# Sixteen engines for w_down's 32 single rows, and a narrow strip of the first values in seven small loads

## The chip, the cores and the metric

The kernel runs on one core of a Trainium2 chip. A core has TensorE (PE in the profile; its weight loads PEld), VectorE (DVE), ScalarE (ACT), GpSimd (POOL) and SyncE (SP), which here only issues transfers, and sixteen DMA engines that carry them out. The metric is the time of one execution on the device in microseconds, the median of several runs.

## The reference

One token of 512 numbers is normalised and goes through two branches in parallel, whose outputs are added to it. All inputs are float32.

```python
xn = layernorm(x)                                   # (1, 1, 512)
# A: attention on a cache, 32 heads of 128, 4096 positions
q = (xn @ wq).reshape(1, 1, 32, 128).transpose(0, 2, 1, 3)
p = softmax(einsum("bhqd,bhkd->bhqk", q, k_cache) * 128 ** -0.5)
a = einsum("bhqk,bhkd->bhqd", p, v_cache) ... .reshape(1, 1, 4096) @ wo
# B: one routed token (the sequence has one), feed-forward width 1376
r = xn @ w_r
y = (silu(xn @ w_gate) * (xn @ w_up)) @ w_down
b = xn + y * sigmoid(r)
return x + a + b
```

The two caches hold 67 MB each; with the weights, 159.5 MB are read once.

## The kernel before

The 32 heads are worked off in eight groups of four. A group's keys (K) and values (V) are 8.39 MB each, 16384 numbers or 64 KB on each of 128 partitions: a partition holds 128 positions of one head. `load_group` (lines 99 to 104) issues such a load as one transfer. Its source is taken apart as `b g p h (c d)`: 32 shares of positions (p) of four heads (h), so that the outermost size of a transfer is 32 and partition 4p + h gets share p of head h.

VectorE and GpSimd multiply keys by the query in place (lines 253, 269) and sum them (264, 271); the softmax's maximum goes over TensorE (324); TensorE multiplies the probabilities by the values, 64 instructions per group (348). There are two places for keys and values in the SBUF: `ring`, with three slots of half a group, for keys of groups 1 to 7 and the last values, and `vals`, with one group, for the keys of group 0 and then for the values of groups 0 to 6. So values g can be loaded once values g-1 are used up, and keys g once VectorE has summed the first half of keys g-1.

All large loads are issued by SyncE in the order in which the program is written: w_q, 32 rows of w_down, keys 0, w_gate and w_up in halves, keys 1, then values g-1 behind keys g, and at the end values 7, the rest of w_down, and w_o in six pieces. A load that is issued waits on each of the sixteen engines behind what was issued earlier.

The framework gives each load one of eight semaphores in turn, DMAHW0 to DMAHW7 (the two tiny loads of x and w_r on ScalarE's queue take part). A load that gets a semaphore again waits on SyncE until the load that had it before has landed; where this is long past, the wait doesn't show in the order of instructions or costs nothing. Waits are also added where a load overwrites something (on the load that wrote it, and on the engines that read it: PE, DVE).

w_down has 1376 rows. The last 1344 are loaded in one piece at the end (`load_down`, line 123). The first T = 32 are loaded at line 133 as single rows into the tile `wf`, one row of 2 KB on each of 32 partitions. `FEW` = 4 sets the outermost size of that transfer's source, `(b a) n -> a b n` with a = 4, and with it which row lies on which partition; lines 296 to 299 put the 32 hidden values that go with them in the same order. TensorE uses both at line 405, near the end.

The main loop (lines 432 to 475) issues keys g and values g-1 ahead of the work on them:

```python
    for g in range(NG + 1):
        if 0 < g < NG:
            K[g] = load_keys(g)
            V[g - 1] = load_group(v_cache, g - 1, vals)
        elif g:
            V[g - 1] = load_group(v_cache, g - 1, ring[:, SLOT:SLOTS * SLOT])
```

Of the kernel before, what the change touches and what calls it, by code (L numbers as in the profile page):

```python
# [14 lines left out]
HP = 4  # L15
# [3 lines left out]
NP = 24  # L19
G = 4  # L20
NCOL = 4
PARTS = (16,), (8, 4, 2.5, 1, 0.5)
T = 32
FEW = 4


@with_exitstack
def kernel(
# [13 lines left out]
    nc = tc.nc  # L42
    _, H, Sk, Dh = k_cache.shape
# [3 lines left out]
    PP = P // HP  # L47
# [5 lines left out]
    RB = BH * Dh // P  # L53
    TH = BH // NCOL
    DC = D // NCOL
    FT = (F - T) // NCOL
    FP = (F - T) * D // P
    QR = NCOL * (F - T) // P
    NS = -(-QR // NCOL)
    OFF = [QR * a // NCOL for a in range(HP)]  # L60
    QC = QB * Dh
# [19 lines left out]
    vals = const.tile([P, 2 * SLOT], F32, name="vals")  # L81
# [14 lines left out]
        halves(t, w.rearrange("(p j) f -> p (j f)", p=P))  # L96
        return [t[:, j * F:(j + 1) * F] for j in range(NK)]

    def load_group(cache, g, t, c0=0):

        n = t.shape[1]
        src = cache[0].rearrange("(b h g) (p c) d -> b g p h (c d)", b=NB, g=GB, p=PP)[g // GB, g % GB]
        nc.sync.dma_start(t, src[:, :, c0 * Dh:c0 * Dh + n])
        return t.rearrange("p (c d) -> p c d", d=Dh)

    def load_keys(g):

        i = (1 - g % 2) * SLOT
        t = load_group(k_cache, g, ring[:, i:i + 2 * SLOT] if g else vals)
        t = [t[:, :HC], t[:, HC:]]  # L110
        return [(h, t[h]) for h in ((1, 0) if g % 2 else (0, 1))]

    def load_wo(t, b, parts):
        src = wo[b * BH * Dh:(b + 1) * BH * Dh, :].rearrange("(p r) n -> p (r n)", p=P)
        x = 0
        for n in parts:
            y = x + int(n * D)
            nc.sync.dma_start(t[:, x:y], src[:, x:y])  # L118
            x = y
        return t.rearrange("p (r n) -> p r n", n=D)  # L120

    def load_down(t):
        nc.sync.dma_start(t, w_down[T:].rearrange("f n -> (f n)").rearrange("(p x) -> p x", p=P))
        return t
# [7 lines left out]
    WF = const.tile([T, D], F32, name="wf")  # L132
    nc.sync.dma_start(WF, w_down[:T].rearrange("(b a) n -> a b n", a=FEW))  # L133
    K, V = {0: load_keys(0)}, {}
# [89 lines left out]
    for j in range(NK):  # L224
        for i in range(NQ * HP):
            t, k = i % NCOL, i // HP
# [12 lines left out]
    def q_part(k):  # L239

        ps = ps_q.tile([P, QB, Dh], F32, name="q")
        nc.tensor.matmul(ps.rearrange("p g d -> p (g d)"), pick.rearrange("p i h -> p (i h)"), q_sb[:, k, :],
                         start=True, stop=True)

        nc.scalar.activation(q_sb[:, k, :], ps.rearrange("p g d -> p (g d)"), AF.Copy)
        return ps
# [4 lines left out]
    def multiply(g, i, c0, c1):  # L251
        q, k = Q[g // QB][:, g % QB, :], K[g][i][1]
        nc.vector.tensor_tensor(  # L253
            k[:, c0:c1, :], k[:, c0:c1, :],
            q[:, None, :].to_broadcast([P, c1 - c0, Dh]), op=ALU.mult
        )

    def sums(g, i):
        if i == 0:
            S[g] = small.tile([P, C], F32, name="s")  # L260
        h, k = K[g][i]
        s = S[g][:, h * HC:(h + 1) * HC]
        for c, n in ((slice(0, HC - NP), Dh), (slice(HC - NP, HC), Dh // 2)):
            nc.vector.tensor_reduce(s[:, c], k[:, c, :n], axis=AX.X, op=ALU.add)  # L264

    def rest(g, i):

        k, q = K[g][i][1][:, HC - NP:], q_sb[:, g // QB, :].rearrange("p (g d) -> p g d", d=Dh)[:, g % QB, :]
        nc.gpsimd.tensor_tensor(k, k, q[:, None, :].to_broadcast([P, NP, Dh]), op=ALU.mult)  # L269
        a, b = k[:, :, :Dh // 2], k[:, :, Dh // 2:]  # L270
        nc.gpsimd.tensor_tensor(a, a, b, op=ALU.add)  # L271
# [18 lines left out]
    def ffn_hidden():  # L290
# [5 lines left out]
        nc.vector.scalar_tensor_tensor(  # L296
            hr[:, NS + 1].rearrange("p (a b) -> p a b", a=FEW), hid[:, :T].rearrange("p (b a) -> p a b", a=FEW), sr,
            up[:, :T].rearrange("p (b a) -> p a b", a=FEW), op0=ALU.mult, op1=ALU.mult,
        )
# [18 lines left out]
    def own_max(g):  # L318
        m = small.tile([P, 1], F32, name="m")
        nc.vector.reduce_max(m, S[g], axis=AX.X)  # L320
        dg = small.tile([P, PP], F32, name="dg")
        nc.vector.tensor_scalar(dg, fold, m, SCALE, op0=ALU.mult, op1=ALU.mult)  # L322
        ps = ps_s.tile([P, 512], F32, name="ps_small")
        nc.tensor.matmul(ps[:, :PP], same.rearrange("p i h -> p (i h)"), dg, start=True, stop=True)  # L324
        MX[g] = ps[:, :PP]

    def head_max(g):
        nm = small.tile([P, 1], F32, name="nm")
        nc.vector.tensor_reduce(nm, MX.pop(g), axis=AX.X, op=ALU.max, negate=True)  # L329
        MX[g] = nm  # L330

    def expo(g):
        nm, s = MX.pop(g), S.pop(g)
        if g % GB == 0:
            RS[g // GB] = small.tile([P, GB], F32, name="rs")
        e = small.tile([P, C], F32, name="e")
        nc.scalar.activation(e, s, AF.Exp, bias=nm, scale=SCALE, accum_out=RS[g // GB][:, g % GB:g % GB + 1])  # L337

        nc.gpsimd.tensor_tensor(PT[g % 2], e[:, :, None].to_broadcast([P, C, HP]),  # L339
                                mine[:, None, :].to_broadcast([P, C, HP]), op=ALU.mult)  # L340

    def values(g):

        v, p, ps = V.pop(g), PT[g % 2], ps_pv[g % 2]
        ng = C // G
        for i in range(ng):
            r = 32 * (i % NCOL)
            nc.tensor.matmul(  # L348
                ps[r:r + M, :], p[:, G * i:G * (i + 1), :].rearrange("p c h -> p (c h)"),
                v[:, G * i:G * (i + 1), :].rearrange("p c d -> p (c d)"),  # L350
                start=(i < NCOL), stop=(i >= ng - NCOL),
            )
# [17 lines left out]
    def turn(b, den):  # L370

        rinv = small.tile([P, TH], F32, name="rinv")
        nc.vector.reciprocal(rinv, den[:, :TH])  # L373
        o = late[2].rearrange("p (r i) -> p r i", r=RB)
        nc.vector.tensor_tensor(
            o.rearrange("p r (k i) -> p k i r", k=TH),
            ps_o.rearrange("p (k i r) -> p k i r", k=TH, r=RB),
            rinv[:, :, None, None].to_broadcast([P, TH, Dh // RB, RB]), op=ALU.mult,
        )
        ot = late[b].rearrange("p (r i) -> p r i", r=RB)  # L380
        nc.vector.transpose(ot.rearrange("p r i -> p (r i)"), o.rearrange("p r i -> p (r i)"))
        OT[b] = ot
# [49 lines left out]
    for g in range(NG + 1):  # L432
        if 0 < g < NG:
            K[g] = load_keys(g)
            V[g - 1] = load_group(v_cache, g - 1, vals)
        elif g:

            V[g - 1] = load_group(v_cache, g - 1, ring[:, SLOT:SLOTS * SLOT])

            WD = load_down(vals[:, :FP])  # L440
            WO = [load_wo(vals[:, SLOT:], 0, PARTS[0]), load_wo(ring[:, :SLOT], 1, PARTS[1])]
            acc = ps_q.tile([P, QB, Dh], F32, name="q").rearrange("p g d -> p (g d)")
            down = ps_q.tile([P, QB, Dh], F32, name="q").rearrange("p g d -> p (g d)")
            for t in (acc, down):
                nc.vector.memset(t, 0.0)
            nc.vector.tensor_copy(acc[0:1, :], base)
        if g:
            own_max(g - 1)
        n = (HC - NP) // 2
        if 0 < g < NG:  # L450
            rest(g, 0)
            multiply(g, 0, 0, n)
        if g:
            head_max(g - 1)
            expo(g - 1)
        if (g + 1) % QB == 0 and (g + 1) // QB < NQ:
            Q[(g + 1) // QB] = q_part((g + 1) // QB)
        if g < NG:
            rest(g, 1)
            if g:  # L460
                multiply(g, 0, n, HC - NP)
                sums(g, 0)
            multiply(g, 1, 0, HC - NP)
            sums(g, 1)
            if DEN:
                turn(*DEN.popitem())
        if g:
            values(g - 1)
            keep(g - 1)
            if g == 1:  # L470
                HL, HF = ffn_hidden()
            if g == NG:
                sb = rows_down()
            if g % GB == 0:
                DEN[g // GB - 1] = collect(g // GB - 1)
# [3 lines left out]
    rows = [(OT[b][:, r, 0:1], WO[b][:, r, :]) for b in range(NB) for r in range(RB)]  # L479
    n = len(rows) - RB + PARTS[1][0]  # L480
    for j, (lhsT, rhs) in enumerate(rows[:n]):
# [6 lines left out]
    for j, (lhsT, rhs) in enumerate(rows[n:-2]):  # L488
        if j == PARTS[1][1]:
            gather(sb, first[:, 0, 0, 0:1])  # L490
# [40 lines left out]
```

## Time and profile before

| | us |
|---|---|
| median of three runs (376.7 to 376.88) | 376.82 |
| the profiled execution | 377.09 |
| its span, first to last instruction | 375.3 |

| engine | busy us | share of the span |
|---|---|---|
| TensorE | 118.3 | 32% |
| VectorE | 228.3 | 61% |
| GpSimd | 172.2 | 46% |
| ScalarE | 16.1 | 4% |

159.45 MB were read, 425 GB/s over the span; the 3814 packets of SyncE's loads took 98.4% of the time of sixteen engines.

In the profile's lists a row gives the line of the kernel, the engine and the operation, then the tile written and those read. In a timeline row the first number is the start, the second the length, both in us from the span's start; "SPq" is SyncE issuing a transfer, and the bracket says how long the engine stood idle before and what ended that. A window row gives the window, its length, each engine's busy time (and instructions), the granted clock of TensorE, and last the share of the sixteen DMA engines' time taken by the packets that begin in the window, and their bytes in GB/s. Since a packet counts where it begins, a share can be above 1.

### The profile page before, as it was taken

What the parts mean: (1) busy time and instruction counts of PE and PEld (TensorE: products, weight loads), DVE (VectorE), ACT (ScalarE), POOL (GpSimd) and SP (SyncE); (2) the same over time, 40 slices, a digit from 0 to 9 for tenths busy, and PEclk for the clock granted to TensorE, in tenths of its full rate; (3) what the DMA queues carried; (4) which work ended last, traced back from release to release, by engine and by line L of the source; (5) the groups of instructions that cost most, each with busy time, mean ns of one, the idle gap of its engine ahead of it and who ended that gap; (6) DMA issues with size and microseconds to landing.
All of it is one profiled execution on the core that took longest, in us unless ns stands there. A gap on an engine that the chain in (4) does not pass through costs nothing.

```text
span 375.3 us, 2071 instructions
## 1 busy us (share of the span) xinstructions
PE 118.3 (32%) x850; PEld 34.9 (9%) x850; DVE 228.3 (61%) x132; ACT 16.1 (4%) x37; POOL 172.2 (46%) x56
## 2 busy tenths in 40 slices
PE   1156045000810063005300490036002700190995
PEld 1101011000200011001000130001000100020222
DVE  6300499389867990699159924995299419970020
ACT  3001000000010000100000000000000000000001
POOL 2000497089407950696059703980299019911000
PEclk9999565555675568556855597559555955575899
DMA  8999899999998999999999999999999999998995
GB/s 336 447 454 447 370 449 447 447 447 440 426 440 385 440 442 433 447 447 447 426 419 405 440 442 433 447 447 435 433 419 420 440 433 433 440 442 387 437 419 219
DMA packets 3826, 159.57 MB, mean 425 GB/s; under 512 B 455, under 2 KB 583, under 8 KB 874
## 3 DMA queue, kind: packets, MB, share of 16 engines
q1 hardware_dynamic: 3814, 159.45, 98.4%
q8 instruction: 6, 0.10, 0.1%
q14 instruction: 2, 0.02, 0.0%
q10 hardware_dynamic: 4, 0.00, 0.0%
HBM read 159.45 MB, written 0.00 MB: 425 GB/s over the span
## 4 chain that ended last, share of the span: by engine, by line
DMA 74%; PE 17%; DVE 7%; SPq 1%; issue 0%; ACT 0%; DVEq 0%
DMA vals<-in_A_v_cache_dram 55%; PE ps_pv L348 17%; DMA vals<-in_A_k_cache_dram 11%; DMA ring<-in_A_wo_dram 9%; DVE s L264 4%; DVE vals L253 3%; SPq L118 0%; PE ps_acc L428 0%; SPq L133 0%; PE ps_small L324 0%; SPq L84 0%; PE ps_o L428 0%; ACT res L499 0%; DVE nm L329 0%; PE ps_pv L428 0%
## 5 line engine op out<-in xcount | busy, mean ns | idle before, releaser
L269 POOL TENSOR_TENSOR ring<-ring,q_sb 128x3072 f32<-128x3072 f32 x14 | 93.6, 6685 | 116.8 <-DMA ring<-in_A_k_cache_dram 116.8
L348 PE MATMUL ps_pv<-vals,pt 128*16 128x512 f32 x448 | 63.0, 726 | 189.4 <-DMA vals<-in_A_v_cache_dram 189.4
L253 DVE TENSOR_TENSOR ring<-ring,q 128x2560 f32<-128x2560 f32 (+1 forms) x21 | 77.8, 3702 | 71.0 <-DMA ring<-in_A_k_cache_dram 71.0
L264 DVE TENSOR_REDUCE s<-ring 128x40 f32<-128x5120 f32 (+1 forms) x28 | 100.0, 3614 | 0.8
L271 POOL TENSOR_TENSOR ring<-ring 128x1536 f32<-128x1536 f32 x14 | 48.1, 3436 | 1.1
L348 PEld LDWEIGHTS ps_pv<-vals,pt 128*16 128x16 f32 x448 | 15.0, 112 | 232.5 <-issue 232.5
L269 POOL TENSOR_TENSOR vals<-vals,q_sb 128x3072 f32<-128x3072 f32 x2 | 13.4, 6689 | 37.6 <-DMA vals<-in_A_k_cache_dram 37.6
L253 DVE TENSOR_TENSOR vals<-vals,q 128x5120 f32<-128x5120 f32 x2 | 11.0, 5483 | 28.3 <-DMA vals<-in_A_k_cache_dram 28.3
L264 DVE TENSOR_REDUCE s<-vals 128x40 f32<-128x5120 f32 (+1 forms) x4 | 14.3, 3614 | 0.1
L373 DVE RECIPROCAL rinv<-ps_small 128x4 f32<-128x4 f32 x2 | 0.4, 178 | 21.5 <-PE ps_small L364 21.5
L227 PE MATMUL ps_pv<-ring,xnT 128*1 128x512 f32 x64 | 9.9, 783 | 10.5 <-DMA ring<-in_A_wq_dram 10.5
L357 ACT ACTIVATE pv<-ps_pv 128x512 f32<-128x512 f32 x8 | 4.8, 597 | 191.5 <-PE ps_pv L348 191.5
L339 POOL TENSOR_TENSOR pt<-e,mine 128x512 f32<-128x512 f32 x8 | 8.3, 1040 | 8.7 <-ACT e L337 8.7
L348 PE MATMUL ps_pv<-ring,pt 128*16 128x512 f32 x64 | 8.4, 687 | 9.4 <-DMA ring<-in_A_v_cache_dram 9.4
L279 PE MATMUL ps_acc<-ring,xnT 128*1 128x336 f32 (+1 forms) x32 | 4.2, 678 | 15.4 <-DMA ring<-in_B_w_gate_dram 15.4
L337 ACT ACTIVATE e<-s,nm 128x128 f32<-128x128 f32 x8 | 3.2, 402 | 120.2 <-DVE nm L329 120.2
L324 PE MATMUL ps_small<-dg,same 128*128 128x32 f32 x16 | 3.6, 309 | 14.4 <-DVE dg L322 14.4
L366 PE MATMUL ps_o<-pv,first 128*128 128x512 f32 x16 | 7.4, 604 | 0.4 <-ACT pv L357 0.4
L271 POOL TENSOR_TENSOR vals<-vals 128x1536 f32<-128x1536 f32 x2 | 6.9, 3450 | 0.2
L279 PE MATMUL ps_o<-ring,xnT 128*1 128x336 f32 (+1 forms) x32 | 5.1, 772 | 3.4 <-DMA ring<-in_B_w_up_dram 3.4
L324 PEld LDWEIGHTS ps_small<-dg,same 128*128 128x128 f32 x16 | 2.9, 218 | 21.4 <-issue 11.9
L198 PE MATMUL ps_small<-ones,pv 1*128 1x1 f32 x8 | 2.0, 370 | 8.3 <-DVE pv L194 8.3
(106 smaller groups left out, 82.4 us busy)
## 6 DMA issues: line engine op xcount, KB each, us to landing
vals<-in_A_wo_dram SPq DMA_DIRECT2D x1, 4096.0 KB, 25.6
ring<-in_B_w_gate_dram SPq DMA_DIRECT2D x2, 1376.0 KB, 44.5
ring<-in_B_w_up_dram SPq DMA_DIRECT2D x2, 1376.0 KB
vals<-in_B_w_down_dram SPq DMA_DIRECT2D x1, 2688.0 KB
ring<-in_A_wo_dram SPq DMA_DIRECT2D x1, 2048.0 KB
ring<-in_A_wo_dram SPq DMA_DIRECT2D x1, 1024.0 KB
ring<-in_A_wo_dram SPq DMA_DIRECT2D x1, 640.0 KB, 32.5
ring<-in_A_wo_dram SPq DMA_DIRECT2D x1, 256.0 KB, 32.7
```

Source lines behind the costliest of these rows:

```text
L227: nc.tensor.matmul(ps_pv[i // NCOL][32 * t:32 * t + 1, :QC], xnT[:, j:j + 1], WQ[j][:, k * QB // GB, i % HP, k % (GB // QB), :], start=(j ...
L253: nc.vector.tensor_tensor(k[:, c0:c1, :], k[:, c0:c1, :], q[:, None, :].to_broadcast([P, c1 - c0, Dh]), op=ALU.mult)
L264: nc.vector.tensor_reduce(s[:, c], k[:, c, :n], axis=AX.X, op=ALU.add)
L269: nc.gpsimd.tensor_tensor(k, k, q[:, None, :].to_broadcast([P, NP, Dh]), op=ALU.mult)
L271: nc.gpsimd.tensor_tensor(a, a, b, op=ALU.add)
L279: nc.tensor.matmul(ps[32 * t:32 * t + 1, a:T + FT], xnT[:, j:j + 1], W[j][:, t * FT + a:T + (t + 1) * FT], start=(j == 0), stop=(j == NK - ...
L324: nc.tensor.matmul(ps[:, :PP], same.rearrange("p i h -> p (i h)"), dg, start=True, stop=True)
L337: nc.scalar.activation(e, s, AF.Exp, bias=nm, scale=SCALE, accum_out=RS[g // GB][:, g % GB:g % GB + 1])
L339: nc.gpsimd.tensor_tensor(PT[g % 2], e[:, :, None].to_broadcast([P, C, HP]), mine[:, None, :].to_broadcast([P, C, HP]), op=ALU.mult)
L348: nc.tensor.matmul(ps[r:r + M, :], p[:, G * i:G * (i + 1), :].rearrange("p c h -> p (c h)"), v[:, G * i:G * (i + 1), :].rearrange("p c d - ...
L357: nc.scalar.activation(PV[g // GB][:, :, g % GB, :], ps_pv[g % 2].rearrange("p (c d) -> p c d", c=G), AF.Copy)
L366: nc.tensor.matmul(ps_o, first[:, c].rearrange("p h i -> p (h i)"), pv[:, c].rearrange("p k d -> p (k d)"), start=(c == 0), stop=(c == G - 1))
```

## The change

The 32 single rows' source gets 16 as its outermost size instead of 4. The load of values 0, and only this, leaves out the last 256 numbers (1 KB) of each partition; these come in seven transfers of their own behind it, each over five of the 32 shares (20 partitions), the last over two (8 partitions).

```diff
+LOW, STRIP = 5, 256
...
-FEW = 4
+FEW = 16
...
-    def load_group(cache, g, t, c0=0):
-
-        n = t.shape[1]
+    def load_group(cache, g, t, c0=0, strip=0):
+
+        n, x = t.shape[1], t.shape[1] - strip
         src = cache[0].rearrange("(b h g) (p c) d -> b g p h (c d)", b=NB, g=GB, p=PP)[g // GB, g % GB]
-        nc.sync.dma_start(t, src[:, :, c0 * Dh:c0 * Dh + n])
+        nc.sync.dma_start(t[:, :x], src[:, :, c0 * Dh:c0 * Dh + x])
+        for p in range(0, PP if strip else 0, LOW):
+            q = min(p + LOW, PP)
+            nc.sync.dma_start(t[p * HP:q * HP, x:], src[p:q, :, c0 * Dh + x:c0 * Dh + n])
         return t.rearrange("p (c d) -> p c d", d=Dh)
...
-            V[g - 1] = load_group(v_cache, g - 1, vals)
+            V[g - 1] = load_group(v_cache, g - 1, vals, strip=STRIP if g == 1 else 0)
```

The order of instructions changes on SyncE alone. In the following rows `A_k_cache` are keys and `A_v_cache` values, the sizes are partitions and numbers on each, and the bracket names the semaphores that the load waits for on SyncE. Before, from the last half of w_up: keys 1, values 0, keys 2, values 1.

```order
L93 DMA ring<-in_B_w_up_dram 64x5504 [waits DMAHW0_49]
L103 DMA ring<-in_A_k_cache_dram 128x1x16384 [waits DMAHW1_49,PE_49]
L103 DMA vals<-in_A_v_cache_dram 128x1x16384 [waits DMAHW4_49,DMAHW2_49,DVE_49]
L103 DMA ring<-in_A_k_cache_dram 128x1x16384 [waits DMAHW3_49,DMAHW5_49,DMAHW1_49,DMAHW6_49,DMAHW0_49,DMAHW7_49,DVE_49,PE_49]
L103 DMA vals<-in_A_v_cache_dram 128x1x16384 [waits DMAHW2_49,PE_49]
```

With the change, the same place:

```order
L94 DMA ring<-in_B_w_up_dram 64x5504 [waits DMAHW0_49]
L104 DMA ring<-in_A_k_cache_dram 128x1x16384 [waits DMAHW1_49,PE_49]
L104 DMA vals<-in_A_v_cache_dram 128x1x16128 [waits DMAHW4_49,DMAHW2_49,DVE_49]
L107 DMA vals<-in_A_v_cache_dram 20x1x256 [waits DMAHW3_49]
L107 DMA vals<-in_A_v_cache_dram 20x1x256
L107 DMA vals<-in_A_v_cache_dram 20x1x256 [waits DMAHW5_49]
L107 DMA vals<-in_A_v_cache_dram 20x1x256 [waits DMAHW6_49]
L107 DMA vals<-in_A_v_cache_dram 20x1x256 [waits DMAHW7_49]
L107 DMA vals<-in_A_v_cache_dram 20x1x256 [waits DMAHW0_49]
L107 DMA vals<-in_A_v_cache_dram 8x1x256 [waits DMAHW1_49]
L104 DMA ring<-in_A_k_cache_dram 128x1x16384 [waits DMAHW2_49,DVE_49,PE_49]
L104 DMA vals<-in_A_v_cache_dram 128x1x16384 [waits DMAHW4_49,DMAHW5_49,DMAHW3_49,DMAHW6_49,DMAHW1_49,DMAHW7_49,DMAHW0_49,PE_49]
```

Seven loads stand between values 0 and keys 2. Values 1 waited on DMAHW2, the semaphore of the values 0 that they overwrite; now keys 2 wait on DMAHW2. Further on, keys 3 to 5 and the values between, before:

```order
L103 DMA ring<-in_A_k_cache_dram 128x1x16384 [waits DMAHW3_49,DVE_49]
L103 DMA vals<-in_A_v_cache_dram 128x1x16384 [waits DMAHW4_49,PE_49]
L103 DMA ring<-in_A_k_cache_dram 128x1x16384 [waits DMAHW5_49,DVE_49]
L103 DMA vals<-in_A_v_cache_dram 128x1x16384 [waits DMAHW6_49,PE_49]
L103 DMA ring<-in_A_k_cache_dram 128x1x16384 [waits DMAHW7_49,DVE_49]
```

and with the change:

```order
L104 DMA ring<-in_A_k_cache_dram 128x1x16384 [waits DMAHW2_49,DVE_49]
L104 DMA vals<-in_A_v_cache_dram 128x1x16384 [waits DMAHW3_49,PE_49]
L104 DMA ring<-in_A_k_cache_dram 128x1x16384 [waits DMAHW4_49,DVE_49]
L104 DMA vals<-in_A_v_cache_dram 128x1x16384 [waits DMAHW5_49,PE_49]
L104 DMA ring<-in_A_k_cache_dram 128x1x16384 [waits DMAHW6_49,DVE_49]
```

The names have moved by one; each load waits for the load that it overwrites (keys for the keys before, values for the values before) and for the engine that reads that.

## The prediction

> **What bounds the kernel now.** I read the page's DMA queues and its chain by engine first, then the chain in order of time, SyncE's timeline, and narrow windows around the places where transfers begin and end. From the page:
>
> ```profile
> q1 hardware_dynamic: 3814, 159.45, 98.4%
> q8 instruction: 6, 0.10, 0.1%
> ...
> DMA 74%; PE 17%; DVE 7%; SPq 1%; issue 0%; ACT 0%; DVEq 0%
> ```
>
> The loads keep sixteen DMA engines busy for 98.4% of the span, so time is lost only where an engine has nothing queued or does something else. q8 is such a thing: six packets of about 16 KB of instructions, 0.1% of 375.3 x 16, or 1 us each. The chain in order of time (start, length) gives the landings of the values:
>
> ```profile
> 68.02 27.48 DMA vals<-in_A_v_cache_dram
> ...
> 95.63 9.43 PE ps_pv L348 x64
> ...
> 105.07 29.02 DMA vals<-in_A_v_cache_dram
> ...
> 297.20 30.05 DMA vals<-in_A_v_cache_dram
> ```
>
> The values of groups 0, 1 and 6 have landed at 95.50, 134.09 and 327.25. Group 1 to 6 are five pairs of an 8.39 MB load of keys and one of values, 38.63 us a pair: 434 GB/s, 27.1 GB/s for each engine, 19.3 us a load. After 327.25 come 19.53 MB (values 7, w_down, w_o), at that rate 45.0 us, to 372.2. The last wait of TensorE ends at
>
> ```profile
> 372.51 0.09 PEld L428 LDWEIGHTS ps_o<-ring 128*1 128x1 f32 x2 [0.22 <-DMA ring<-in_A_wo_dram]
> ```
>
> So whichever engine is last at 95.50 runs from there to the end without a gap, and its lateness at 95.50 is lateness of the kernel. Which engines are late shows in windows around the end of values 0; a packet of these loads is 64 KB per partition, so bytes per window count the engines that take up the next load:
>
> ```profile
> core 0: us, PE busy (x) PEld busy (x) DVE busy (x) ACT busy (x) POOL busy (x), PEclk, DMA share, GB/s
> 92.90:94.30 1.40, 0.00 (x0) 0.00 (x0) 1.40 (x1) 0.00 (x0) 1.32 (x2) 0.50 1.63 702
> 94.30:95.00 0.70, 0.00 (x0) 0.00 (x0) 0.67 (x2) 0.00 (x0) 0.70 (x1) 0.50 0.00 0
> 95.00:95.20 0.20, 0.00 (x0) 0.00 (x0) 0.20 (x1) 0.00 (x0) 0.20 (x1) 0.50 0.76 328
> 132.40:133.30 0.90, 0.00 (x0) 0.00 (x0) 0.86 (x2) 0.00 (x0) 0.82 (x2) 0.50 0.00 0
> 133.30:133.80 0.50, 0.00 (x0) 0.00 (x0) 0.50 (x1) 0.00 (x0) 0.50 (x1) 0.50 0.61 262
> ```
>
> 702 GB/s in 1.40 us is 983 KB, fifteen packets; 328 in 0.20 is one. Fifteen engines begin keys 2 between 92.9 and 94.3, one at 95.1. One round later 262 in 0.50 us is two: another engine has dropped back. Nobody stops in between, because keys 2 lie queued long before. SyncE's timeline:
>
> ```profile
> 68.02 0.55 SPq L103 DMA_DIRECT2D vals<-in_A_v_cache_dram  x1
> 89.19 0.54 SPq L103 DMA_DIRECT2D ring<-in_A_k_cache_dram  x1
> 105.07 0.54 SPq L103 DMA_DIRECT2D vals<-in_A_v_cache_dram  x1
> 127.68 0.54 SPq L103 DMA_DIRECT2D ring<-in_A_k_cache_dram  x1
> ```
>
> Keys 2 go out at 89.19, 3.7 us before the first engine runs dry.
>
> **The change, part by part.** *The balance.* w_down's 32 single rows of 2 KB lay on four engines, eight each. On sixteen it is two each: 4 KB at 27.1 GB/s, +0.15 us on twelve engines, -0.45 on four. The strip takes 1 KB off each of an engine's eight rows of values 0, 8 KB or -0.30 us on all. The seven loads give five engines 24 or 28 rows of 1 KB. A row's price is in the last 0.25 us of the loads, when one engine is left (the window 371.85:372.10 below): 20 GB/s x 0.25 us are five rows, 0.05 us each. So five engines get +1.2 to +1.4, net between +0.45 and +1.25; eleven get -0.15. Which engines they are, no view tells. All but one engine were at least 0.8 us ahead at 94.3, so even the most loaded one of these comes to 94.3 + 1.25 = 95.5, about level with the last. If nothing else happened, the end would move by -0.15 to about +0.1.
>
> The Trainium skill (DMA: Bandwidth & Descriptors, "Why a DMA increments its semaphore by 16 and not by 1") says a copy uses the largest number of engines up to sixteen that divides both outer sizes, and the lowest-numbered ones: five, five times more, and two. No run here shows the numbers.
>
> *The new wait.* The semaphores of the loads go round in eights, and a load waits until the last one on its semaphore has landed. Values 0 have DMAHW2 before and after. Before, keys 2 were the next load, on DMAHW3; now seven loads stand between, and keys 2 get DMAHW2 again. Their row has that wait new, and values 0 themselves had already waited on this semaphore for its earlier user, so what is new must be the landing of values 0's main part. SyncE cannot issue keys 2 at 89.19 any more, only after 95.50 + 0.15 - 0.30 = 95.35. By then fifteen engines stand still. Behind keys 2 on SyncE's queue are only values 1, which go out at 105.07 as before, when TensorE's 9.43 us on values 0 end. The strips are hidden: the first six go out behind values 0, the seventh waits for keys 1 (landed by 76.3 below), and their 1.4 us on five engines fall into the standstill.
>
> What the standstill costs is bounded by the two places where the queue is empty in this trace. One is the start of w_q, also 8.39 MB on sixteen engines; SyncE, windows, and the page's line of its issue (last number: us to landing):
>
> ```profile
> 0.73 0.40 SPq L84 DMA_DIRECT2D ring<-in_A_wq_dram  x1
> ```
>
> ```profile
> 0.73:1.70 0.97, 0.00 (x0) 0.00 (x0) 0.71 (x4) 0.19 (x1) 0.80 (x5) 1.00 0.01 2
> 1.70:2.90 1.20, 0.00 (x0) 0.00 (x0) 1.09 (x3) 1.09 (x1) 1.04 (x5) 1.00 2.49 874
> 2.90:4.80 1.90, 0.00 (x0) 0.00 (x0) 1.80 (x10) 0.00 (x0) 0.06 (x1) 1.00 0.00 0
> 4.80:5.60 0.80, 0.00 (x0) 0.00 (x0) 0.73 (x3) 0.00 (x0) 0.42 (x3) 1.00 3.04 1311
> ```
>
> ```profile
> ring<-in_A_wq_dram SPq DMA_DIRECT2D x1, 22.2
> ```
>
> Sixteen packets begin 1.0 to 2.2 us after the issue (874 x 1.20 = 1049 KB) and the next sixteen from 4.8 on, so a first packet takes about 3 us and not 2.4, and the engines are spread over up to 0.8 us. From issue to landing it is 22.2 us, 2.9 more than 19.3. With it, keys 2 land at 95.37 + 22.2 = 117.57. Before they landed just ahead of
>
> ```profile
> 76.29 2.82 DVE L253 TENSOR_TENSOR ring<-ring,q 128x2560 f32<-128x2560 f32 x1 [7.71 <-DMA ring<-in_A_k_cache_dram]
> ...
> 114.82 2.82 DVE L253 TENSOR_TENSOR ring<-ring,q 128x2560 f32<-128x2560 f32 x1 [2.13 <-DMA ring<-in_A_k_cache_dram]
> ```
>
> at 114.82 (keys 1 ahead of 76.29): **+2.75 us**. The other place is the store at the end:
>
> ```profile
> 373.28 0.28 SPq L502 DMA_DIRECT2D out_dram<-res  x1
> ```
>
> ```profile
> 373.28:373.95 0.67, 0.00 (x0) 0.00 (x0) 0.00 (x0) 0.00 (x0) 0.00 (x0) 1.00 0.00 0
> 373.95:374.10 0.15, 0.00 (x0) 0.00 (x0) 0.00 (x0) 0.00 (x0) 0.00 (x0) 1.00 0.04 14
> ```
>
> Its packet begins 0.7 us after the issue. With that and full rate at once, keys 2 land at 95.37 + 0.7 + 19.3 + 0.4 (from a packet's end to its landing: the last engine went on at 95.0 to 95.2, the landing was 95.50) = 115.8: +1.0. A gain is excluded, since no engine can begin before 95.37 and the last one began at 95.1. I take w_q's, the same size and number of engines, and keep +1.0 and, for an issue 0.14 us longer (0.54 against 0.40), +2.9 as ends.
>
> The Trainium skill (DMA: Bandwidth & Descriptors, "Latency and other measured facts") gives about 0.6 us to the first byte from SyncE. The store's 0.7 agrees, w_q's 1.0 to 2.2 does not; by the page the standstill would cost +0.9.
>
> *What the standstill does to the late engines.* Before, only the last engine's lateness counts; the six instruction packets of q8 that fell on other engines only brought these up towards it. The windows at the end of the loads (rows of 1 and 2 KB):
>
> ```profile
> 369.60:370.00 0.40, 0.39 (x16) 0.10 (x12) 0.00 (x0) 0.20 (x1) 0.00 (x0) 1.00 1.02 399
> ...
> 370.35:370.55 0.20, 0.20 (x18) 0.19 (x12) 0.00 (x0) 0.05 (x1) 0.00 (x0) 1.00 0.62 251
> ...
> 370.70:371.10 0.40, 0.40 (x20) 0.23 (x11) 0.00 (x0) 0.00 (x0) 0.00 (x0) 1.00 0.50 195
> ...
> 371.40:371.55 0.15, 0.05 (x4) 0.05 (x8) 0.00 (x0) 0.00 (x0) 0.00 (x0) 1.00 0.42 150
> 371.85:372.10 0.25, 0.25 (x16) 0.16 (x4) 0.00 (x0) 0.00 (x0) 0.00 (x0) 1.00 0.06 20
> ```
>
> Share x 16 is the number of engines still at work: sixteen until 370, ten at 370.45, eight at 370.9, seven at 371.5, one at 372.0. Two groups of eight, one ending around 370.3, the other around 371.7: 1.4 us apart, the price of one instruction packet (1 us of its own and what its neighbours on the engine lose). At 95 only one engine was apart, so the others were set back later. After the change all sixteen wait for the late engine at 95.35 and start together, and the engines set back after that are late on top of it. The engine that restarted last is 0.8 us behind the first; an engine set back by 1.4 ends 0.6 (if it restarted first) to 1.4 (if last) behind it. With five or so such engines the worst lies above the middle: **+1.1 us**.
>
> The Trainium skill (Runtime: NRT & Kernel Launch, "Instruction fetch mechanics") says that instructions come in blocks of 16 KiB and that this is mostly hidden. q8's packets agree in size; the two groups say that it is not hidden from a queue of loads that is always full. By the page this term would be nothing, the whole +2.75.
>
> *Nothing else moves.* Keys 3 wait for VectorE's sums of keys 2 (issue 127.68, 12.9 after its first instruction on keys 2), so 2.75 later, while values 1 now end over 19 us after 117.57. From there the order of issues and waits is the old one. The other reading order of the hidden row's first 32 values is one VectorE instruction while VectorE has 2 us to spare ahead of 114.82.
>
> The sum: the profiled execution took 377.09 us (span 375.3 and 1.8 around it); 377.09 + 2.75 + 1.1 = 380.94. The median is 0.27 lower, 376.82, so **380.7 us**, 1.0% slower. The ends are +1.0 + 0.6 = +1.6 (378.4) and +2.9 + 1.4 = +4.3 (381.1).
>
> **Rivals.** *Cheap restart.* Alone on an idle queue keys 2 start as quickly as the store did, and the late engines are not the worst: 378.4 to 379.8, about 379.1. For it: w_q started while four more issues came behind it, the chip was cold. Against: same size, same engines. The page's 0.6 us, named above, would fall in here. Chance 0.13.
>
> *Not slower: the wait is met early.* The one mechanism that saves the change is that keys 2 wait for something old on DMAHW2 and still go out by 92.9, when the first engine would run dry; from there on each microsecond counts. Then only the balance is left: the late engine -0.15 us, 376.7, no change, or 376.9 if one of the five loaded engines is last. For it: a row of the order names a semaphore, not the count. Against: values 0 already waited on it. Should the rows still lie on four engines, it would be 376.5. Chance 0.09.
>
> *Two setbacks on one engine.* With the engines together, two instruction packets on one make it 1.4 us later again: 382.1. For it: six packets on sixteen engines, in no order that a view shows; against: the end shows two groups, no third. Chance 0.06.
>
> **How the numbers follow.** The forecast (379.8 to 381.7) has 0.72. The range 379.0 to 381.8 adds the upper half of the cheap restart and leaves out what lies below, the not slower case and most of the double setback. Within 0.2% (0.75 us) is what this measurement cannot tell from no change: 0.07, nearly all of the not slower case; faster 0.02, its remainder; slower 0.91.
>
> **What would show it.** In SyncE's timeline keys 2 at 95.4 and not 89.2. In windows no packet of keys 2 before 96, the DMA share near nothing for over a microsecond on most engines, sixteen packets from 96.4 to 97.6. VectorE's first instruction on keys 2 at 117.6 (115.8 for the cheap restart, 114.7 if the wait is met early). Values landing every 38.6 us from then on up to the engine that is set back, then later. At the end a group of engines 1.4 us behind. I am wrong if keys 2 go out at 89, if the first landing after them is late by less than 1 us, or if the last landing is late by no more than keys 2 were.

## The result, and the profile after

The changed kernel is slower: it took 381.55 and 381.76 us against 376.79 for the kernel before (median, 376.70 to 376.88): 1.0129 times, 95% interval 1.0105 to 1.0153. Two more runs of it took 389.87 and 394.10 (with them its median is 385.81), but single runs of several kernels here, the one before too, come out far above the rest, and the comparisons below leave them out, save one run in each of the two ratios of the six strips (382.58 and 383.02 us), which are 0.001 to 0.002 too high by it. The profiled execution took 381.55 us, its span 379.7, 4.4 more than before.

The page of the changed kernel: as many bytes, the sixteen engines busy for a smaller share, and the same six packets of 16 KB of instructions on queue q8. Each of these is called a block below.

```profile
q1 hardware_dynamic: 3986, 159.45, 97.6%
q8 instruction: 6, 0.10, 0.1%
```

SyncE's timeline (start, length) around the change. Keys 2 were issued at 89.19 before; they go out at 95.27 now, and the loads behind them later, except values 1:

```profile
67.70 0.55 SPq L104 DMA_DIRECT2D vals<-in_A_v_cache_dram  x1
68.31 8.29 SPq L107 DMA_DIRECT2D vals<-in_A_v_cache_dram  x7
95.27 0.59 SPq L104 DMA_DIRECT2D ring<-in_A_k_cache_dram  x1
104.91 0.57 SPq L104 DMA_DIRECT2D vals<-in_A_v_cache_dram  x1
131.08 0.54 SPq L104 DMA_DIRECT2D ring<-in_A_k_cache_dram  x1
```

Windows of the changed kernel (the last two columns are the DMA engines' share and GB/s of the packets that begin there):

```profile
94.60:96.60 2.00, 1.32 (x8) 0.37 (x12) 2.00 (x1) 0.00 (x0) 2.00 (x1) 0.50 0.00 0
96.60:97.00 0.40, 0.40 (x8) 0.06 (x4) 0.40 (x1) 0.00 (x0) 0.40 (x1) 0.50 7.37 2294
97.00:98.20 1.20, 1.20 (x12) 0.33 (x8) 1.20 (x1) 0.00 (x0) 0.37 (x1) 0.50 0.25 109
98.20:99.60 1.40, 1.40 (x12) 0.29 (x8) 1.40 (x1) 0.00 (x0) 0.00 (x0) 0.50 0.00 0
99.60:101.00 1.40, 1.40 (x16) 0.33 (x12) 1.40 (x2) 0.00 (x0) 0.00 (x0) 0.74 1.73 749
```

No packet begins for two microseconds: this is the standstill. Then 2294 GB/s x 0.40 us, 918 KB, are fourteen packets of 64 KB within 0.4 us; two stragglers follow, and all sixteen engines begin their second packet between 99.6 and 101.0. The first fourteen took 7.37 x 0.40 x 16 / 14 = 3.4 us each. The time from the issue of keys 2 to their landing is called the restart. VectorE's first instruction on keys 2, at 114.82 before, and TensorE's last wait, at 372.51 before, in two timelines of the changed kernel:

```profile
118.22 2.82 DVE L257 TENSOR_TENSOR ring<-ring,q 128x2560 f32<-128x2560 f32 x1 [5.70 <-DMA ring<-in_A_k_cache_dram]
```

```profile
376.88 0.09 PEld L432 LDWEIGHTS ps_o<-ring 128*1 128x1 f32 x2 [0.19 <-DMA ring<-in_A_wo_dram]
```

Of the 4.37 us at the end, 3.40 are there when keys 2 land and 0.97 come after. Where the 0.97 come from is in the chain, in order of time:

```profile
104.91 32.59 DMA vals<-in_A_v_cache_dram
...
146.55 30.11 DMA vals<-in_A_v_cache_dram
...
186.60 28.66 DMA vals<-in_A_v_cache_dram
...
224.68 29.40 DMA vals<-in_A_v_cache_dram
```

Values 1 to 4 land at 137.50, 176.66, 215.26 and 254.08. The steps are 39.16, 38.60 and 38.82 us, where every step before was 38.6. The DMA queues in the window 137.5 to 157.4 of the changed kernel show what is in the longest one:

```profile
q8 instruction: 1, 0.02, 0.3%
```

One block falls into this step, none into the second and one into the third. What a block does to its engine shows in two narrow windows of the changed kernel:

```profile
140.95:141.00 0.05, 0.05 (x4) 0.00 (x0) 0.05 (x1) 0.00 (x0) 0.00 (x0) 0.50 1.10 328
141.75:141.87 0.12, 0.12 (x7) 0.00 (x0) 0.12 (x1) 0.00 (x0) 0.00 (x0) 1.00 1.55 546
```

The first holds the block alone: 328 x 0.05 are 16 KB, in 1.10 x 0.05 x 16 = 0.9 us. The second holds the one packet of 64 KB (546 x 0.12) that begins as the block ends, and it takes 1.55 x 0.12 x 16 = 3.0 us instead of 2.4. So a block sets its engine back by about 1.4 us.

### The profile page after: what moved, and what is told of

It is laid out like the page before. It is cut to its first block, busy times and chain, and to the rows that moved or that the text cites. A ratio compares the mean times of both kernels' runs of the same rounds, so it can differ in the third digit from the quotient of the medians.

```text
span 379.7 us, 2081 instructions
## 1 busy us (share of the span) xinstructions
PE 120.3 (32%) x850; PEld 35.4 (9%) x850; DVE 228.3 (60%) x132; ACT 16.1 (4%) x37; POOL 172.1 (45%) x56
## 4 chain that ended last, share of the span: by engine, by line
DMA 73%; PE 20%; POOL 5%; issue 1%; SPq 0%; ACTq 0%; ACT 0%; DVE 0%; POOLq 0%
DMA vals<-in_A_v_cache_dram 47%; PE ps_pv L352 17%; DMA ring<-in_A_k_cache_dram 11%; DMA ring<-in_A_wo_dram 9%; DMA ring<-in_A_wq_dram 6%; POOL ring L273 4%; PE ps_pv L231 3%; POOL ring L275 1%; POOL pt L343 0%; PE ps_acc L432 0%; SPq L122 0%; PE ps_small L328 0%; ACTq L530 0%; ACT res L503 0%; DVE nm L333 0%
## 5 line engine op out<-in xcount | busy, mean ns | idle before, releaser
L352 PE MATMUL ps_pv<-vals,pt 128*16 128x512 f32 x448 | 64.8, 744 | 191.6 <-DMA vals<-in_A_v_cache_dram 165.3
L352 PE MATMUL ps_pv<-ring,pt 128*16 128x512 f32 x64 | 9.7, 775 | 9.9 <-DMA ring<-in_A_v_cache_dram 9.9
L283 PE MATMUL ps_o<-ring,xnT 128*1 128x336 f32 (+1 forms) x32 | 4.0, 639 | 3.3 <-DMA ring<-in_B_w_up_dram 3.3
```

The costliest lines, as they stand in the source:

```text
L283: nc.tensor.matmul(ps[32 * t:32 * t + 1, a:T + FT], xnT[:, j:j + 1], W[j][:, t * FT + a:T + (t + 1) * FT], start=(j == 0), stop=(j == NK - ...
L352: nc.tensor.matmul(ps[r:r + M, :], p[:, G * i:G * (i + 1), :].rearrange("p c h -> p (c h)"), v[:, G * i:G * (i + 1), :].rearrange("p c d - ...
```

## The experiments

**The rows alone.** Only `FEW = 16`; no strip.

```diff
-FEW = 4
+FEW = 16
```

> Only the 32 single rows of w_down over sixteen engines, no strip. Theory (all of the loss is the new wait of keys 2): no wait is new, keys 2 go out at 89.2 us and land by 114.8 to 115.0; the late engine carries 4 KB more, so 376.8 to 377.0. Rival (the rows' new spread costs part of the 4.8 us): 378 or more.

It took 376.97 us, ratio 0.9999 (0.999 to 1.0008); keys 2 went out at 89.02 and VectorE began on them at 114.66. The single rows neither cost nor gain anything that can be measured.

**The wait alone.** The kernel before with seven tiny loads behind values 0, into a tile that nothing uses.

```diff
-    const.tile([P, 96], F32, name="gap")
+    gap = const.tile([P, 96], F32, name="gap")
...
             V[g - 1] = load_group(v_cache, g - 1, vals)
+            for i in range(7 if g == 1 else 0):
+                nc.sync.dma_start(gap[i:i + 1, :], w_r.rearrange("(o n) -> o n", o=1)[:, :96])
```

> The kernel before with seven loads of 384 bytes each (part of w_r into an unused tile) between values 0 and keys 2: the wait without strip and without spread rows. Theory: keys 2 wait for the landing of values 0 (95.5 us), are issued at 95.5 and land at 118.2 to 118.6; 381 to 382.2, the whole loss. Rival (strip or rows cost it): 376.8 to 377.2.

381.35 us, ratio 1.0119 (1.0105 to 1.0132): the whole loss, without strip and without spread rows. SyncE's timeline of this kernel, and VectorE's:

```profile
68.72 7.38 SPq L437 DMA_DIRECT2D gap<-in_B_w_r_dram  x7
95.22 0.55 SPq L103 DMA_DIRECT2D ring<-in_A_k_cache_dram  x1
```

```profile
118.23 2.82 DVE L253 TENSOR_TENSOR ring<-ring,q 128x2560 f32<-128x2560 f32 x1 [5.54 <-DMA ring<-in_A_k_cache_dram]
```

Keys 2 are issued within 0.05 us, and used within 0.01 us, of the times in the changed kernel.

**One tiny load fewer.** The same with `range(6 ...)`.

> The kernel before with six such tiny loads, the same but for one. Theory: keys 2 wait for keys 1, long landed; issued at 89.2; 376.8 to 377.1. Rival (any small load behind values 0 holds up the queue, by about 0.6 us each): 380.

376.99 us, ratio 0.9993 (0.9973 to 1.0013); keys 2 at 88.86. Six loads of the same kind in the same place cost nothing, the seventh 4.4 us. So it is the semaphore that keys 2 get, and not a load, that makes them wait.

**The strip without the wait.** Both parts of the change with six loads, `LOW, STRIP = 6, 256`, so that keys 2 get another semaphore.

> Both parts of the change, but the strip in six loads of six shares (the last of two) instead of seven of five; keys 2 then get the semaphore of keys 1, landed at 76. Theory: keys 2 go out at 89.2 again, no standstill, only the balance is left: 376.5 to 376.9. Rival (the small loads and their rows of 1 KB cost the time): 380 to 382 as with seven.

Keys 2 went out at 89.07 and were used from 114.91 on: no standstill. But it took 377.2 to 377.9 us, ratio 1.003 (0.9994 to 1.0065), not the 376.5 to 376.9 that the theory wanted. By itself the interval still holds "no change", so the strip was run once more, with the rows left on four engines (`FEW = 4`):

> The strip in six loads of six shares and w_down's single rows on four engines as before: the strip without the wait and without the spread rows. Theory (what kept the kernel with both at 377.7 and not at 376.8 is the strip: its 1 KB rows slow the first packets of keys 2 on all engines by 0.3 to 0.4 us): 377.2 to 378.0, keys 2 landed by 115.0 to 115.4. Rival (it was the spread rows together with the strip): 376.7 to 377.0.

377.89 us, ratio 1.0045 (1.0015 to 1.0075): the strip alone costs a good microsecond instead of gaining 0.3. VectorE began on keys 2 at 115.50, 0.7 later than before. (With the rows spread too, it began only 0.25 later than with the rows alone, and the rest of that loss came behind keys 2; why it came later there was not tried.) The place shows in the windows around the end of values 0. First the rows alone, then the six strips with spread rows:

```profile
92.00:94.30 2.30, 0.00 (x0) 0.00 (x0) 2.30 (x1) 0.00 (x0) 2.22 (x2) 0.50 1.05 456
```

```profile
92.00:94.30 2.30, 0.00 (x0) 0.00 (x0) 2.30 (x1) 0.00 (x0) 2.22 (x2) 0.50 1.31 484
```

Without the strip 456 x 2.30 = 1049 KB are sixteen packets of 64 KB in 1.05 x 2.30 x 16 = 38.6 us, 2.4 us each. With it 484 x 2.30 = 1113 KB are 128 rows of 1 KB and fifteen such packets, in 48.2 us; with 0.05 us for a row (the price from the end of the kernel before) 41.8 us are left, 2.8 for a packet. So beside the small rows the large packets of the other engines run slower too. In the changed kernel the strip falls ahead of the first packets of keys 2, into the standstill, which is why the wait alone costs as much as the whole change.

**The wait late.** The seven tiny loads behind values 5 (`if g == 6`), so that keys 7 have to wait for values 5.

> The kernel before with the seven tiny loads between values 5 and keys 7 instead of behind values 0: the same wait late, with two blocks of instructions still to come instead of five. Theory (a standstill costs its restart wherever it stands, plus what the blocks after it do): keys 7 go out at 288.6 and land at 311.3 to 311.6 (307.9 before), the end is 3.6 to 4.2 us later than before, 380.5 to 381.1, a little less than with the early wait (381.35). Rival (the cost is in what the early loads do to each other, of the first two groups): under 379.

381.47 us, ratio 1.0122 (1.0107 to 1.0137), more than the theory wanted, although keys 7 landed earlier than it said (310.8 and not 311.3 to 311.6). SyncE's and VectorE's timelines of this kernel, and VectorE's of the kernel before at the same place:

```profile
288.38 0.55 SPq L103 DMA_DIRECT2D ring<-in_A_k_cache_dram  x1
```

```profile
310.82 2.82 DVE L253 TENSOR_TENSOR ring<-ring,q 128x2560 f32<-128x2560 f32 x1 [15.70 <-DMA ring<-in_A_k_cache_dram]
```

```profile
307.97 2.82 DVE L253 TENSOR_TENSOR ring<-ring,q 128x2560 f32<-128x2560 f32 x1 [12.61 <-DMA ring<-in_A_k_cache_dram]
```

Keys 7 are 2.85 us late, and since the span is 4.3 us longer (379.6 against 375.3), some 1.4 come after, with two blocks of instructions still to come. The rival, that only the first groups suffer, is out. The setback did not get smaller with fewer blocks.

**Fewer instructions for TensorE.** To see what the blocks of instructions do, TensorE was given less to fetch: one matmul in `values` instead of 32 (`for i in range(1)`), in both kernels. 31 of 32 products of probabilities and values are left out; all loads stay.

> The kernel before with only the first of the 32 matmuls of probabilities by values in each group (31 of 32 left out), so that TensorE runs through about 1000 instructions fewer and fetches about four blocks of instructions fewer, most of those after 95 us. Theory (before, only the engine that is late at 95 counts, and it owes that to the block at 53 us, which stays): values 7 land at 346.5 as in the kernel before, 376.7 to 377.1. Rival (each block of instructions costs the end something in any kernel): about 376.

> The changed kernel with the same 31 of 32 matmuls of each group left out. Theory (after the standstill all engines are equal, and every later block of instructions pushes the end): keys 2 land at 118.2 as in the changed kernel, values 7 at 349.9 to 350.1 and not 350.8, because no block comes between; the end is 380.2 to 381.2, depending on the one block that is left near the end, against 381.6. Rival (the blocks do nothing, the loads restart in a worse order after the standstill): values 7 at 350.8 and 381.6.

The kernel before so cut took 376.92 us, ratio 1.0 (0.999 to 1.0009): the blocks that it no longer fetches after 95 us (one is left) gain nothing there. The changed one took 381.57, ratio 1.0122 (1.0105 to 1.0139), where 380.2 to 381.2 were expected. Values 7 had landed at 350.0 as the theory said, without a slip on the way, but one block was still fetched at 360 us, and that alone brought the end back to where five had put it (TensorE's last wait at 376.94, with five at 376.88). The setbacks do not add up; one suffices.

So more was cut: three of four matmuls of each `collect`, seven of the eleven in `rows_down`, and all products with w_o but those of the last two rows.

> The kernel before with so much of TensorE's work left out that no block of its instructions should be fetched between the one at 53 to 60 us and the end: 31 of 32 matmuls of probabilities by values in each group, three of four of each collection of heads, seven of eleven of w_down's large part, and all products with w_o but those of the last two rows. All loads stay. Theory: the engine that the early block set back is last all the way, as in the kernel before: 376.5 to 377.0. Rival (the end owes something to the later blocks): under 376.3.

> The changed kernel with the same work left out. Theory (two terms: the restart, 3.4 us at keys 2, and one setback by a block after it, 1.0 us however many come): keys 2 land at 118.2, values 7 at 350.0, and the last piece of w_o at 375.8 instead of 376.9 in the last two changed kernels; 380.3 to 380.7, 3.4 to 3.8 above the same cut of the kernel before. Rival (the blocks do not matter, the restart costs all): 381.4 to 381.7.

The cut kernel before took 377.05 us, ratio 1.0004 (0.9994 to 1.0013), as expected. The cut changed one took 381.88, ratio 1.013 (1.0115 to 1.0145), not 380.3 to 380.7: one block was fetched all the same, at 369 us. With it in the way the run could not decide, and a last cut took out what was left ahead of that block (the rest of w_down's large part, `join` and `gather`):

> The cut changed kernel with a little more of TensorE's work left out (w_down's large part, and the adding up of its result and of the first group's), so that the one block that was still fetched at 369 us is not needed before the end. Theory (the setback by a block is a term of its own): from the first half of w_o's second part on nothing moves any more; the last piece lands 9.8 us after its first half as in the cut kernel before, at 376.1 to 376.3 and not 376.9, 381.0 to 381.2 against 381.88. Rival (the blocks do not matter): 381.7 to 381.9.

381.25 us, ratio 1.0114 (1.0097 to 1.0131), 0.6 less than with the block, or 0.4 when each is taken against its own runs of the kernel before (376.84 and 377.03); the theory had wanted 0.7 to 0.9. In the profile the effect is clean. TensorE's timeline from values 7 to the last half row but one of w_o, with the block (the three fences are the cut changed kernel with it, the one without it, and the cut kernel before):

```profile
350.42 1.87 PE L352 MATMUL ps_pv<-ring,pt 128*16 128x512 f32 x2 [10.45 <-DMA ring<-in_A_v_cache_dram]
...
376.02 0.37 PE L432 MATMUL ps_acc<-ring 128*1 128x128 f32 x1 [10.14 <-DMA ring<-in_A_wo_dram]
```

```profile
362.63 1.86 PE L352 MATMUL ps_pv<-ring,pt 128*16 128x512 f32 x2 [10.46 <-DMA ring<-in_A_v_cache_dram]
387.54 0.37 PE L432 MATMUL ps_acc<-ring 128*1 128x128 f32 x1 [18.25 <-DMA ring<-in_A_wo_dram]
```

```profile
346.28 1.86 PE L348 MATMUL ps_pv<-ring,pt 128*16 128x512 f32 x2 [10.45 <-DMA ring<-in_A_v_cache_dram]
...
371.16 0.37 PE L428 MATMUL ps_acc<-ring 128*1 128x128 f32 x1 [9.43 <-DMA ring<-in_A_wo_dram]
```

25.60, 24.91 and 24.88 us for the same bytes. (In the second kernel's profile keys 2 were issued at 107.67 instead of 95.31, hence its late times; only differences within it are used, and from 120 to 360 us it ran at 433 GB/s.) The block costs the changed kernel 0.7 us here. The cut kernel before fetches a block in this stretch too, at 364 us, and pays nothing, so it must have fallen on an engine that was ahead.

Without a block the loss is still 4.2 us (381.25 against 377.05). Nearly all of that is there when keys 2 land. VectorE's first instruction on them in the cut changed kernel with the block, where keys 2 were issued at 95.31, and in the cut kernel before:

```profile
118.62 2.82 DVE L257 TENSOR_TENSOR ring<-ring,q 128x2560 f32<-128x2560 f32 x1 [10.68 <-DMA ring<-in_A_k_cache_dram]
```

```profile
114.48 2.82 DVE L253 TENSOR_TENSOR ring<-ring,q 128x2560 f32<-128x2560 f32 x1 [6.71 <-DMA ring<-in_A_k_cache_dram]
```

That is 4.14 later, and not 3.40 as in the changed kernel. From there to TensorE's last wait it is 257.61 us in the cut kernel before, 257.62 in the kernel without a block and 258.34 in the one with it: behind the restart nothing is lost unless a block comes. Why the restart itself was longer shows on the second queue of instructions, q14, whose packets have 8 KB; the prediction did not count them. One falls into keys 2 of the cut changed kernel (first line, for 109.9 to 113.4 us):

```profile
q14 instruction: 1, 0.01, 0.6%
...
110.30:110.40 0.10, 0.00 (x0) 0.00 (x0) 0.00 (x0) 0.00 (x0) 0.00 (x0) 0.50 1.84 655
116.70:117.50 0.80, 0.00 (x0) 0.00 (x0) 0.00 (x0) 0.00 (x0) 0.00 (x0) 0.50 2.84 1229
117.50:118.10 0.60, 0.00 (x0) 0.00 (x0) 0.00 (x0) 0.00 (x0) 0.00 (x0) 0.50 0.00 0
118.10:118.20 0.10, 0.00 (x0) 0.00 (x0) 0.00 (x0) 0.00 (x0) 0.00 (x0) 0.50 1.52 655
```

It takes 0.3 us (0.6% of 3.5 x 16), and a packet of 64 KB that begins between 110.3 and 110.4 takes 1.84 x 0.10 x 16 = 2.9 us instead of 2.4. Fifteen engines (1229 x 0.80 = 983 KB) are through with keys 2 and begin the next load by 117.5, the last only after 118.1: two packets of 2.4 us behind that long one. So here too one engine out of step keeps all waiting, by 0.6 us or more.

No version came out faster than the kernel before: of the two parts of the change, one does nothing and the other costs a microsecond even without the wait.

## Why the prediction was right, and where it was off

380.7 us were forecast, with 379.0 to 381.8; 381.55 and 381.76 were measured. By the steps:

- **The new wait: right.** Keys 2 at 95.37 forecast, 95.27 measured, and the tiny loads show that the wait is the whole cause.
- **Values 0 land at 95.35: right by luck.** They landed just ahead of the issue at 95.27. But with the tiny loads, without any strip, the issue came at 95.22, so the strip saved nothing; the time fits because this execution was 0.3 ahead from the start (keys 1 used at 75.99, 76.29 before). And the step that led there, eight rows of 63 KB save 0.30 us and small rows burden only the engines that carry them, was wrong in its second half: without the standstill the strip costs about 1 us, since the large packets beside it take 2.8 us instead of 2.4. The forecast of 376.7 for "not slower, the wait is met early" should have been 377.7. This did not reach the sum, because the standstill covers the strip.
- **The restart, +2.75 us from w_q's 22.2: too small.** From the issue to VectorE's use it took 118.22 - 95.27 = 22.95 us, so +3.40. First packets begin 1.3 us after the issue instead of 1.0 and take 3.4 us instead of 3. That is the term that was mis-sized, by 0.65, more than the whole miss of the profiled execution (381.55 against 380.94). Its upper end, +2.9, was too low as well: w_q's start was taken for the dear case since the chip was cold there. In the late wait it was 22.4 us from issue to use, so w_q's 22.2 is the lower end of what the runs show, and the store's quick start did not carry over to a load on sixteen engines. Some of the 22.95 is not the start: one 8 KB packet of q14 falls into keys 2 of the changed kernel too, and again fifteen engines are through by 117.6 and one after 117.7 (windows below). None falls into the late wait.

```profile
116.60:117.60 1.00, 0.00 (x0) 0.00 (x0) 0.00 (x0) 0.00 (x0) 0.00 (x0) 0.50 2.28 983
117.70:117.80 0.10, 0.00 (x0) 0.00 (x0) 0.00 (x0) 0.00 (x0) 0.00 (x0) 0.50 1.52 655
```

- **The late engines, +1.1: right in size and kind, wrong in one particular.** 0.97 came after keys 2. That only the worst engine counts is confirmed by the cut kernels, but it need not be the worst of "five or so": a single block cost 0.9 us at 360 us and 0.7 at 369, five cost 0.97, the two behind the late wait 1.4. What was taken as a maximum over several is nearly the same for a single one.
- **Nothing else moves: right.** Keys 3 went out at 131.08, 3.40 after their 127.68, as keys 2 landed 3.40 later.

The sum was near because the restart was taken too low by 0.65 and the setback too high by 0.13; the measured terms make 377.09 + 3.40 + 0.97 = 381.46, and the profiled execution took 381.55.

## What to carry to other kernels

Where a framework hands out a few semaphores in turn, the number of loads between two large ones decides what the second one waits for: a seventh small load here made a prefetch wait for the load just ahead of it, and the queue that was always full ran dry. Before a transfer is cut into pieces, look which later transfer will get whose semaphore. A standstill of a queue on sixteen engines costs more than its own length: all engines then start level, so that leads that had absorbed later disturbances are gone.

## What the runs showed of the hardware

- An 8.39 MB load that starts on idle engines needs 22.2 (w_q) to 22.4 us (keys 7 in the late wait) from issue to landing, against 19.3 behind another load; 22.95 and 23.31 where 8 KB of instructions came in between.
- A block of 16 KB of instructions sets the engine that carries it back by about 1.4 us: 0.9 of its own and 0.5 to 0.6 on the next packet. It shows in the total only when it makes that engine the last: cutting all but one of the blocks after 95 us left the kernel before at 1.0 times its time, while a single block at 369 us cost the cut changed kernel 0.7 us.
- 128 rows of 1 KB, in six loads, slowed the 64 KB packets that ran beside them from 2.4 to 2.8 us. What in the memory or the engines does this was not tried.
